# First four groups of a windowed-attention and MLP kernel in another order of work

## The chip, the cores and the metric

The kernel runs on one core of a Trainium2 chip: TensorE (PE in the profile, its weight loads PEld), VectorE (DVE), ScalarE (ACT), GpSimd (POOL), SyncE (SP, here only a DMA queue) and 16 DMA engines. The metric is device time of one execution in microseconds; the median of the runs is compared.

## The reference

Four sequences of 768 tokens, 8 heads of 64, attend causally to a window of 128 tokens and to the first 4 tokens of the sequence (the sinks). The result, 3072 tokens by 512, goes through two matrix products with a quick GELU between them. Input and output are float32.

```python
scores = scale * np.matmul(q, k.transpose(0, 1, 3, 2))
keep = is_sink | ((rel >= 0) & (rel < window))
scores = np.where(keep, scores, -1000000000.0)
a = np.exp(scores - np.max(scores, axis=-1, keepdims=True))
a = a / (np.sum(a, axis=-1, keepdims=True) + 1e-09)
x = np.matmul(a, v)              # then (tokens, heads * head_dim)
h = x @ w_in
return (h * (1.0 / (1.0 + np.exp(-1.702 * h)))) @ w_out
```

## The kernel before

The 3072 tokens are cut into 12 groups of 256 (three to a sequence, `NT`), a group into two blocks of 128 tokens, and the 8 heads into four pairs, `hp`. Everything is written for fp16 operands; loads on POOL's queue convert. The schedule is manual: each engine executes its instructions in the order in which the program text issues them, and waits by semaphores for tiles of other engines. So the order of the calls is the order of work, and a waiting instruction holds up all that follow on its engine or its queue.

For a group, the steps are functions of the same names as in the diff. `load_part` issues one of six loads on POOL (two each of q, k and v). `transposed_qk` brings q and k to the layout with features on partitions: groups 0 to 2 (`EARLY` is 3) by transposes on TensorE with copies by DVE and ACT, the others by one DMA transpose on SP's queue. `sinks` and `scores` are the first matmuls on it, `maxima` (DVE) merges the window's two blocks by a mask and takes row maxima, `weights` (ACT) are four exponentials, `weights_transposed` turns them (TensorE and a copy for groups 0 and 1, a DMA transpose on SP after that), `lower` (DVE) and `upper` (POOL) mask the two halves, `values` multiplies by v, and `normal` (DVE) divides. `sink_terms`, `sink_weights`, `sink_transposed` do the same for the sinks. `x_transposed` turns the result for the products: on TensorE for groups 0 and 1, by DMA for the others. `ahead(n, hp)` is `sinks` (for pair 0), `scores` and `maxima` of a pair.

The products are `hidden(g, F2)`, eight blocks of 8 matmuls, each followed by a GELU on ACT, and `o(g, i, parts)`, four quarters of four matmuls for each of two token blocks, ended by `out_store`. Exponentials and GELU need different tables on ACT, which loads one at each change.

PSUM has eight banks: tag `nat` holds two score tiles of two banks, `mm` two banks (products, some transposes), `av` two banks (values, sink scores, other transposes). A tile waits until the previous holder of its buffer has been read.

Before the main loop stand the attention of group 0 and, between its steps, most of that of group 1. The main loop then runs stage n: exponentials of group n and the output products of group n-2 with its last two pairs of scores, then the hidden products of group n-1 with, between them, the values of group n and the first scores of group n+1. The DMA transpose of q and k of group n+2 is issued in stage n; for n = 1, which has a form of its own (`first`), `transposed_qk(3)` closes the stage. The start of stage n in its common form:

```python
            if att:
                for hp in (0, 1):
                    weights(n, hp)
                    weights_transposed(n, hp)
            o(g2, 0, 0, 1, 2, 3)
...
                weights(n, 3)
                weights_transposed(n, 3)
                sink_weights(n)
                lower(n, 0)
                if n + 2 < NG:
                    transposed_qk(n + 2)
```

## Time and profile before

| what | us |
|---|---|
| median of 3 runs | 249.29 (248.48 to 249.64) |
| the profiled execution, its own time | 249.51 |
| span of its trace | 247.8 |
| TensorE busy in the span | 222.1 (90%) |
| DVE, ACT, POOL busy | 148.0, 154.3, 99.9 |

In the profile a row of the timeline gives the start, the duration, the engine, the line, the operation with its result and operands, and in square brackets the idle time before it and what ended it. Rows with the letter q behind an engine's name are its sequencer's, among them the issues of DMAs. A window's row gives, for a stretch of time, the length, the busy time of the chosen engine, the granted clock of TensorE (1.00 is full), how busy the DMA engines were and the GB/s that they moved.

### The profile page before, as it was taken

Reading aid. Unit: us, or ns where it says so; the run is one execution under the profiler, and the core shown is the slowest. Engines: PE = TensorE matmul, PEld = TensorE weight load, DVE = VectorE, ACT = ScalarE, POOL = GpSimd, SP = SyncE. Lnnn points to the kernel's source line nnn. Section 1 sums busy time; section 2 is a strip of 40 time slices with the busy share of each in tenths; the row PEclk is TensorE's granted clock in tenths of the full one; section 3 lists DMA queues with packets and bytes.
Section 4 is the critical chain, followed back from the end, with each engine's and each line's share of the span. In section 5 each row is a group of like instructions: output and inputs, shape, how many; then the busy total and the mean of one; then the engine's idle time right before and its main releaser. Section 6 shows DMA issues by size and latency. Waiting matters only on the chain.

```text
span 247.8 us, 5720 instructions
## 1 busy us (share of the span) xinstructions
PE 222.1 (90%) x2172; PEld 151.8 (61%) x2172; DVE 148.0 (60%) x390; ACT 154.3 (62%) x350; POOL 99.9 (40%) x152
## 2 busy tenths in 40 slices
PE   0654779699999999999999999999999999799993
PEld 0542559548748649558478477487485694594851
DVE  7679725847757478379577467586682783730101
ACT  2286476277667775875775776677668757751430
POOL 8988594407622616637235276156110210310000
PEclk9996559999999999999999999999999999999999
DMA  9999999999999999999989989999992513503102
GB/s 81 152 197 198 163 207 182 154 127 174 178 146 131 158 169 142 130 202 160 129 165 122 163 150 159 160 144 143 157 157 43 139 33 68 147 3 85 42 3 86
DMA packets 134668, 33.13 MB, mean 134 GB/s; under 512 B 127344, under 2 KB 131568, under 8 KB 134640
## 3 DMA queue, kind: packets, MB, share of 16 engines
q0 software_dynamic: 79104, 13.64, 72.6%
q1 hardware_dynamic: 55104, 18.99, 43.8%
q8 instruction: 17, 0.28, 0.5%
q10 hardware_dynamic: 432, 0.13, 0.2%
q14 instruction: 11, 0.09, 0.1%
HBM read 27.50 MB, written 6.29 MB: 136 GB/s over the span
## 4 chain that ended last, share of the span: by engine, by line
PE 63%; DMA 13%; DVE 10%; ACT 8%; issue 3%; SPq 2%; ACTq 0%; DVEq 0%
PE hT L387 30%; PE o L402 20%; DMA xT<-xn 9%; ACT A L251 4%; DVE m L236 3%; DVE nat L232 3%; PE nat L220 2%; DMA AT<-A 2%; PE av L339 2%; ACT L390 2%; PE av L327 2%; PE av L335 2%; PE tA L264 2%; DMA vsr<-in_v_dram 2%; SPq L424 1%
## 5 line engine op out<-in xcount | busy, mean ns | idle before, releaser
L387 PE MATMUL hT<-xT,w_in 128*128 128x256 f16 x768 | 95.5, 275 | 3.2 <-ACT gT L390 1.7
L402 PE MATMUL o<-w_out,gT 128*128 128x512 f16 x384 | 88.3, 380 | 0.0
L387 PEld LDWEIGHTS <-w_in 128*128 128x128 f16 x768 | 72.9, 99 | 16.4 <-DMA xT<-xn 2.6
L390 ACT ACTIVATE gT<-hT 128x512 f16<-128x512 f32 x96 | 56.2, 597 | 42.3 <-PE hT L387 42.2
L251 ACT ACTIVATE A<-nat,bias 128x128 f16<-128x128 f32 x192 | 53.8, 376 | 26.2 <-DVE bias L240 23.0
L313 POOL TENSOR_SCALAR_AFFINE_SELECT up<-AT 128x512 f16<-128x512 f16 (+1 forms) x48 | 28.0, 594 | 92.0 <-DMA AT<-A 86.8
L402 PEld LDWEIGHTS <-gT 128*128 128x128 f16 x384 | 35.2, 98 | 39.9
L232 DVE COPY_PREDICATED nat<-prev,nat 128x512 f32<-128x512 uint16 x48 | 33.2, 692 | 30.0 <-ACT A L251 13.1
L236 DVE TENSOR_REDUCE m<-nat 128x4 f32<-128x512 f32 x48 | 33.2, 691 | 1.6
L123 POOL DMA_DIRECT2D qkn<-in_q_dram x24 | 21.6, 910 | 5.0 <-DMA w_out<-in_moe_w_out_dram 3.3
L410 DVE COPY osb<-o 128x512 f32<-128x512 f32 x12 | 8.3, 690 | 23.7 <-PE o L402 23.7
L123 POOL DMA_DIRECT2D qkn<-in_k_dram x24 | 21.3, 895 | 1.9 <-DMA w_in<-in_moe_w_in_dram 1.6
L123 POOL DMA_DIRECT2D vn<-in_v_dram x24 | 21.3, 895 | 1.6 <-issue 1.1
L357 DVE TENSOR_TENSOR xn<-av,rcp 128x256 f16<-128x256 f32 x48 | 20.4, 424 | 1.7
L300 DVE TENSOR_TENSOR lo<-AT,own 128x512 f16<-128x512 f16 (+1 forms) x48 | 18.9, 413 | 2.1 <-DMA AT<-A 2.1
L335 PE MATMUL av<-vn,up 128*128 128x65 f16 x160 | 18.3, 195 | 0.0
L339 PE MATMUL av<-vn,lo 128*128 128x65 f16 x160 | 18.3, 196 | 0.0
L356 DVE RECIPROCAL rcp<-av 128x4 f32<-128x4 f32 x48 | 8.6, 179 | 14.6 <-PE av L339 14.4
L220 PEld LDWEIGHTS <-qkT 64*128 64x128 f16 x352 | 11.5, 99 | 8.5 <-issue 8.1
L327 PE MATMUL av<-vs,AsT 128*128 128x130 f16 x80 | 16.5, 224 | 0.0
L220 PE MATMUL nat<-qkT 64*128 64x128 f16 x288 | 16.0, 228 | 0.0
L335 PEld LDWEIGHTS <-up 128*128 128x128 f16 x160 | 14.8, 100 | 0.6 <-issue 0.2
(51 smaller groups left out, 168.2 us busy)
## 6 DMA issues: line engine op xcount, KB each, us to landing
out_dram<-osb SPq DMA_DIRECT2D x24, 256.0 KB
qkn<-in_q_dram POOLq DMA_DIRECT2D x24, 128.0 KB, 5.3
qkn<-in_k_dram POOLq DMA_DIRECT2D x24, 128.0 KB, 5.0
vn<-in_v_dram POOLq DMA_DIRECT2D x24, 128.0 KB, 5.5
w_in<-in_moe_w_in_dram POOLq DMA_DIRECT2D x4, 512.0 KB, 9.1
w_out<-in_moe_w_out_dram POOLq DMA_DIRECT2D x4, 512.0 KB, 10.6
AT<-A SPq DMA_TRANSPOSE x40
xT<-xn SPq DMA_TRANSPOSE x10
```

What stands on the lines that cost most here:

```text
L123: nc.gpsimd.dma_start(dst, (q, k, v)[e][b, :, rows].rearrange("h s d -> s h d"))
L220: nc.tensor.matmul(o, qkT[r, 0, i, hp], keys[r], start=True, stop=True)
L232: nc.vector.copy_predicated(out=nat[:, :, :, P:], mask=kinds(take_prev, g % NT), data=nat[:, :, :, 0:P])
L236: nc.vector.tensor_reduce(out=m1.rearrange("p h i -> p (h i)"), in_=nat.rearrange("p h i c -> p (h i) c")[:, :, P:], axis=AX.X, op=ALU.max,)
L251: nc.scalar.activation(out=A[:, 2 * h + i], in_=nat[:, h, i, P:], func=AF.Exp, bias=bias[:, i, hp, h : h + 1], scale=scale,)
L313: nc.gpsimd.affine_select(out=out, in_=in_, pattern=[[0, rows], [-1, P]], compare_op=ALU.is_gt, fill=zero_reg, base=0, channel_multiplier=1,)
L327: nc.tensor.matmul(av[:, i].rearrange("p h d -> p (h d)"), AsT, vs[b][:, c : c + 2].rearrange("p h d -> p (h d)"), start=True, stop=False,)
L335: nc.tensor.matmul(av[:, i, h], up[:, h, i], vn[b][J // 2][:, J % 2, head], start=False, stop=False)
L339: nc.tensor.matmul(av[:, i, h], own_w[:, h, i], vn[b][t][:, i, head], start=(I == 0), stop=(I == 0 or h == 1))
L387: nc.tensor.matmul(hT[:, f], w_in16[:, c, bass.ts(F, P)], xT[:, :, c], start=(c == 0), stop=(c == 3))
L390: nc.scalar.activation(out=G[g]["gT"][:, 2 * F2 : 2 * F2 + 2].rearrange("p f s -> p (f s)"), in_=hT.rearrange("p f i s -> p (f i s)"), fun ...
L402: nc.tensor.matmul(o, gT[:, F, bass.ts(i, P)], w_out16[:, F], start=(F == 0), stop=(F == NF - 1))
```

## The change

The main loop begins at group 3 (`EARLY`) and loses the form for n = 1. Ahead of it groups 0 to 2 are written out. Group 0's attention runs by itself until its x is transposed; the hidden products of group 0 carry the second half of group 1's q and k transposes and three pairs of its scores, those of group 1 the same for group 2. The third pair has its two halves in the two `av` banks, so that three pairs of scores wait for their exponentials at once. The output products of a group are cut into quarters with the next group's weights, values and normalisation between them. The exponentials and the scores of group 3 stand beside the output products of group 1, with group 2's values.

Group 1's weights are transposed on TensorE into score buffers, two pairs at a time. x of group 2 is transposed on TensorE. `lower` of the first two pairs of group 0 moves to POOL (`selected`). The `vs` and `vn` constants are set later, but for those of the first sequence and group. The first chunk of w_in is loaded ahead of group 1's q and k, the output weights after group 0's masks; the loads of groups 2 to 5 move as the diff shows. On SP's queue, q and k of group 3 are transposed behind `out_store` of group 0, those of groups 4 and 5 both behind the weights of group 3.

```diff
@@ -154,14 +154,14 @@
         else:
             for part in parts:
                 for a in (2 * part, 2 * part + 1):
-                    bank = mm_bank if g < 2 else av_bank
-                    tp = bank(f"tqk{g}_{a}", (P, HP, P), FP16)
+                    first = g == 0 or (g == 1 and part == 0)
+                    tp = (mm_bank if first else av_bank)(f"tqk{g}_{a}", (P, HP, P), FP16)
                     for c in range(HP):
                         nc.tensor.transpose(tp[:, c], n[:, a, bass.ts(c, P)], ident)
-                    if a % 2 == 0:
+                    if (g == 1 and part == 0) or (g != 1 and a % 2 == 1):
+                        nc.scalar.copy(T[:, bass.ts(a, HP)], tp)
+                    else:
                         nc.vector.tensor_copy(out=T[:, bass.ts(a, HP)], in_=tp)
-                    else:
-                        nc.scalar.copy(T[:, bass.ts(a, HP)], tp)
...
-        nat = psp.tile([P, 2, 2, 2 * P], FP32, tag="nat", bufs=2, name=f"nat{g}_{hp}")
+        if (g, hp) in ((1, 2), (2, 2)):
+            nat = [av_bank(f"nat{g}_{hp}_{h}", (P, 2, 2 * P)) for h in range(2)]
+        else:
+            whole = psp.tile([P, 2, 2, 2 * P], FP32, tag="nat", bufs=2, name=f"nat{g}_{hp}")
+            G[g]["whole", hp] = whole
+            nat = [whole[:, h] for h in range(2)]
...
-                    o = nat[:, h, i, bass.ts(part, P)]
+                    o = nat[h][:, i, bass.ts(part, P)]
...
     def maxima(g: int, hp: int):
         m1 = work.tile([P, 2, 2], FP32, tag="m1", name=f"m1{g}_{hp}")
+        if ("whole", hp) in G[g]:
+            nat = G[g]["whole", hp]
+        else:
+            for h, nat in enumerate(G[g]["nat", hp]):
+                nc.vector.copy_predicated(
+                    out=nat[:, :, P:], mask=kinds(take_prev, g % NT)[:, h], data=nat[:, :, 0:P]
+                )
+                nc.vector.tensor_reduce(out=m1[:, h], in_=nat[:, :, P:], axis=AX.X, op=ALU.max)
...
-    def weights_transposed(g: int, hp: int):
-        A = G[g]["A", hp]
+    def flat_weights(g: int, hp: int):
         AT = work.tile([P, 2, 2, P], FP16, tag="AT", bufs=6, name=f"AT{g}_{hp}")
-        flat = AT.rearrange("p h i s -> p (h i) s")
-        if g < 2:
+        G[g]["AT", hp] = AT
+        return AT.rearrange("p h i s -> p (h i) s"), G[g]["A", hp]
+
+    def weights_transposed(g: int, hp: int, copy=None):
+
+        flat, A = flat_weights(g, hp)
+        if copy is not None:
             tp = mm_bank(f"tA{g}_{hp}", (P, 4, P), FP16)
             for a in range(4):
                 nc.tensor.transpose(tp[:, a], A[:, a], ident)
-            if g == 0 or hp < 3:
-                nc.scalar.copy(flat, tp)
-            else:
-                nc.vector.tensor_copy(out=flat, in_=tp)
+            copy(flat, tp)
         else:
             nc.sync.dma_start_transpose(flat, A.rearrange("p a c -> p (a c)"))
-        G[g]["AT", hp] = AT
+
+    def two_weights_transposed(g: int, pairs, copy):
+
+        tp = psp.tile([P, 2, 8, P], FP16, tag="nat", bufs=2, name=f"tA{g}_{pairs[0]}")
+        for e, hp in enumerate(pairs):
+            flat, A = flat_weights(g, hp)
+            for a in range(4):
+                nc.tensor.transpose(tp[:, e, a], A[:, a], ident)
+            copy(flat, tp[:, e, 0:4])
+
+    def by_dve(out_, in_):
+        nc.vector.tensor_copy(out=out_, in_=in_)
+
+    def by_act(out_, in_):
+        nc.scalar.copy(out_, in_)
...
-    def lower(g: int, hp: int):
+    def lower(g: int, hp: int, pool=False):
 
         AT, i0 = G[g]["AT", hp], int(g % NT == 0)
         lo = work.tile([P, 2, 2, P], FP16, tag="lo", bufs=4, name=f"lo{g}_{hp}")
...
+        if pool:
+            selected(lo, AT, i0, 1)
+        else:
+            nc.vector.tensor_tensor(
+                out=lo[:, :, i0:], in0=AT[:, :, i0:], op=ALU.mult,
+                in1=own.unsqueeze(1).unsqueeze(1).broadcast_to((P, 2, 2 - i0, P)),
+            )
         G[g]["lo", hp] = lo
 
     def upper(g: int, hp: int):
         AT, i0 = G[g]["AT", hp], int(g % NT == 0)
         up = work.tile([P, 2, 2, P], FP16, tag="up", bufs=4, name=f"up{g}_{hp}")
+        selected(up, AT, i0, -1)
+        G[g]["up", hp] = up
+
+    def selected(to, AT, i0: int, sign: int):
...
+            out=out, in_=in_, pattern=[[0, rows], [sign, P]], compare_op=ALU.is_gt if sign < 0 else ALU.is_ge,
+            fill=zero_reg, base=0, channel_multiplier=-sign,
         )
...
-        if g < 2:
+        if g < EARLY:
...
-                if g == 0 or i == 0:
+                if i == 0:
                     nc.scalar.copy(xT[:, bass.ts(i, HP)], tp)
                 else:
                     nc.vector.tensor_copy(out=xT[:, bass.ts(i, HP)], in_=tp)
...
-    def out_store(g: int, i: int):
+    def out_store(g: int, i: int, act=False):
         b, t = divmod(g, NT)
         osb = work.tile([P, DM], FP32, tag="osb", bufs=3, name=f"osb{g}_{i}")
-        if i == 0:
+        if i == 0 or act:
             nc.scalar.copy(osb, G[g]["o", i])
         else:
             nc.vector.tensor_copy(out=osb, in_=G[g]["o", i])
...
-    for i in range(2):
-        for b in range(B):
+    for b in range(B):
+        for i in range(2):
             nc.sync.dma_start(vsr[bass.ts(i, 32), b], v[b, :, 0:n_sink])
     masked_l = const.tile([P, P], FP16, name="maskedl")
     masked_r = const.tile([P, P], FP16, name="maskedr")
+    sinkA = [const.tile([P, P], FP16, name=f"sinkA{i}") for i in range(2)]
+    nc.vector.memset(vs[0], 0.0)
+    nc.vector.tensor_copy(out=vs[0][:, :, D : D + 1], in_=sink_rows.unsqueeze(2))
     nc.vector.memset(masked_l, -1000.0)
-    for row in vn:
-        for t_ in row:
-            nc.vector.memset(t_[:, :, :, D : D + 1], 1.0)
-    sinkA = [const.tile([P, P], FP16, name=f"sinkA{i}") for i in range(2)]
-    for t_ in (*kd, *sinkA, *vs):
+    for t_ in (*kd, *sinkA):
         nc.vector.memset(t_, 0.0)
-    for t_ in vs:
-        nc.vector.tensor_copy(out=t_[:, :, D : D + 1], in_=sink_rows.unsqueeze(2))
+    nc.vector.memset(vn[0][0][:, :, :, D : D + 1], 1.0)
     zero_reg = nc.gpsimd.to_reg(0.0)
+    load_w_in(0)
     load_qk(1)
     load_v(0)
-    load_w_in(0)
-    load_w_in(1)
-    transposed_qk(0)
-    sink_keys(0, nc.vector.tensor_copy)
-    load_v(1)
-    load_w_in(2)
-    load_w_in(3)
-    load_qk(2)
+    for i in (1, 2, 3):
+        load_w_in(i)
+
+    def sink_columns(b: int):
+        nc.vector.memset(vs[b], 0.0)
+        nc.vector.tensor_copy(out=vs[b][:, :, D : D + 1], in_=sink_rows.unsqueeze(2))
...
+    transposed_qk(0, (0,))
+    sink_values(0)
+    transposed_qk(0, (1,))
+    sink_keys(0, nc.vector.tensor_copy)
     ahead(0, 0)
     ahead(0, 1)
     weights(0, 0)
-    transposed_qk(1, (0,))
     weights(0, 1)
-    transposed_qk(1, (1,))
     scores(0, 2)
+    weights_transposed(0, 0, by_act)
     maxima(0, 2)
-    weights_transposed(0, 0)
+    upper(0, 0)
+    lower(0, 0, pool=True)
+    weights(0, 2)
     scores(0, 3)
     maxima(0, 3)
     sink_terms(0)
-    weights(0, 2)
-    weights_transposed(0, 1)
+    weights_transposed(0, 1, by_act)
+    upper(0, 1)
+    lower(0, 1, pool=True)
+    sink_weights(0)
     weights(0, 3)
-    ahead(1, 0)
-    weights_transposed(0, 2)
-    sink_weights(0)
-    sink_values(0)
-    lower(0, 0)
-    lower(0, 1)
-    ahead(1, 1)
-    weights_transposed(0, 3)
     sink_transposed(0)
-    upper(0, 0)
-    upper(0, 1)
-    load_v(2)
+    weights_transposed(0, 2, by_dve)
+    lower(0, 2)
     upper(0, 2)
+    weights_transposed(0, 3, by_act)
+    values(0, 0)
+    values(0, 1)
+    transposed_qk(1, (0,))
+    normal(0, 0)
+    lower(0, 3)
     upper(0, 3)
+    normal(0, 1)
+    for hp in (2, 3):
+        values(0, hp)
+        normal(0, hp)
+    x_transposed(0)
     load_w_out(0)
     load_w_out(1)
-    lower(0, 2)
-    lower(0, 3)
+    load_v(1)
+    load_w_out(2)
+    load_w_out(3)
+    load_qk(2)
+
+
+    for F2 in range(NF // 2):
+        hidden(0, F2)
+        if F2 == 0:
+            transposed_qk(1, (1,))
+            for row in vn:
+                for t_ in row[int(row is vn[0]) :]:
+                    nc.vector.memset(t_[:, :, :, D : D + 1], 1.0)
+        if F2 in (1, 2, 3):
+            ahead(1, F2 - 1)
+
+
     weights(1, 0)
-    weights_transposed(1, 0)
     weights(1, 1)
-    weights_transposed(1, 1)
-    for hp in range(HP):
-        values(0, hp)
-        if hp == 1:
-            scores(1, 2)
-        if hp == 3:
-            scores(1, 3)
-        normal(0, hp)
-        if hp == 1:
-            maxima(1, 2)
-            weights(1, 2)
-    weights_transposed(1, 2)
-    x_transposed(0)
+    sink_columns(1)
+    o(0, 0, 0)
+    o(0, 1, 0)
+    scores(1, 3)
     maxima(1, 3)
     sink_terms(1)
+    o(0, 0, 1)
+    weights(1, 2)
+    two_weights_transposed(1, (0, 1), by_dve)
+    sink_weights(1)
     weights(1, 3)
-    weights_transposed(1, 3)
-    load_w_out(2)
-    load_w_out(3)
+    upper(1, 0)
+    upper(1, 1)
+    o(0, 1, 1)
+    sink_transposed(1)
+    lower(1, 0)
+    lower(1, 1)
+    o(0, 0, 2)
+    two_weights_transposed(1, (2, 3), by_act)
+    upper(1, 2)
+    upper(1, 3)
+    values(1, 0)
+    normal(1, 0)
+    values(1, 1)
+    lower(1, 2)
+    normal(1, 1)
+    o(0, 1, 2)
+    lower(1, 3)
+    values(1, 2)
+    normal(1, 2)
+    o(0, 0, 3)
+    values(1, 3)
+    normal(1, 3)
+    out_store(0, 0)
+    o(0, 1, 3)
+    x_transposed(1)
+    out_store(0, 1, act=True)
+    load_v(2)
     load_qk(3)
-
-    for n in range(1, NG + LAG2):
-        att, first = n < NG, n == 1
+    load_v(3)
+
+
+    for F2 in range(NF // 2):
+        hidden(1, F2)
+        if F2 in (0, 1):
+            transposed_qk(2, (F2,))
+        if F2 in (2, 3, 4):
+            ahead(2, F2 - 2)
+    transposed_qk(3)
+    sink_keys(1, nc.gpsimd.tensor_copy)
+
+
+    for hp in (0, 1):
+        weights(2, hp)
+        weights_transposed(2, hp)
+    sink_values(1)
+    o(1, 0, 0, 1, 2)
+    scores(2, 3)
+    maxima(2, 3)
+    sink_terms(2)
+    weights(2, 2)
+    weights_transposed(2, 2)
+    o(1, 0, 3)
+    out_store(1, 0)
+    ahead(3, 0)
+    load_part(4, 0)
+    upper(2, 0)
+    load_part(4, 1)
+    upper(2, 1)
+    o(1, 1, 0)
+    sink_weights(2)
+    weights(2, 3)
+    weights_transposed(2, 3)
+    lower(2, 0)
+    lower(2, 1)
+    load_part(4, 2)
+    upper(2, 2)
+    load_part(4, 3)
+    upper(2, 3)
+    o(1, 1, 1)
+    sink_transposed(2)
+    weights(3, 0)
+    weights_transposed(3, 0)
+    scores(3, 1)
+    lower(2, 2)
+    maxima(3, 1)
+    o(1, 1, 2)
+    for hp in (0, 1):
+        values(2, hp)
+        normal(2, hp)
+    scores(3, 2)
+    weights(3, 1)
+    weights_transposed(3, 1)
+    lower(2, 3)
+    values(2, 2)
+    normal(2, 2)
+    o(1, 1, 3)
+    out_store(1, 1, act=True)
+    values(2, 3)
+    normal(2, 3)
+    maxima(3, 2)
+    x_transposed(2)
+    scores(3, 3)
+    maxima(3, 3)
+    sink_terms(3)
+    weights(3, 2)
+    weights_transposed(3, 2)
+    weights(3, 3)
+    weights_transposed(3, 3)
+    sink_weights(3)
+    load_qk(5)
+    lower(3, 0)
+    transposed_qk(4)
+    transposed_qk(5)
+    sink_columns(2)
+    sink_columns(3)
+
+    for n in range(EARLY, NG + LAG2):
+        att = n < NG
...
+        if n > EARLY:
+            if att and n + 1 < NG and (n + 1) % NT == 0:
+                sink_keys((n + 1) // NT, nc.gpsimd.tensor_copy)
+            if n in (4, 5):
+                load_v(n)
             if att:
                 for hp in (0, 1):
...
-            if first:
-                upper(n, 2)
-                upper(n, 3)
-                load_v(3)
-                load_qk(4)
-                load_v(4)
-            else:
-                for part in range(4):
-                    if n + 3 < NG:
-                        load_part(n + 3, part)
-                    if part < 2:
-                        upper(n, 2 + part)
+            for part in range(4):
+                if n + 3 < NG:
+                    load_part(n + 3, part)
+                if part < 2:
+                    upper(n, 2 + part)
...
-                if first:
-                    lower(n, 0)
-            if first and F2 in (2, 3):
-                transposed_qk(2, (F2 - 2,))
-            if F2 == (6 if first else 1):
                 ahead(n + 1, 0)
-            if F2 == 1:
                 lower(n, 1)
-            if F2 == (7 if first else 1):
...
-            for hp, at in enumerate((4, 5, 6, 7) if first else (3, 4, 6, 7)):
+            for hp, at in enumerate((3, 4, 6, 7)):
                 if F2 == at:
...
-                    if not first and hp in (1, 2):
+                    if hp in (1, 2):
                         paced_load(n + 3, 3 + hp, n, hp)
         if att:
             x_transposed(n)
             if n + 1 < NG and (n + 1) % NT == 0:
                 sink_values((n + 1) // NT)
-            if first:
-                transposed_qk(3)
-
```

## Prediction

> **What bounds the kernel now.** I read the page first, then the chain of waits, then the timeline engine by engine for the first 95 us, and last the half-microsecond windows of DMA traffic.
>
> ```profile
> PE 222.1 (90%) x2172; PEld 151.8 (61%) x2172; DVE 148.0 (60%) x390; ACT 154.3 (62%) x350; POOL 99.9 (40%) x152
> PEclk9996559999999999999999999999999999999999
> PE hT L387 30%; PE o L402 20%; DMA xT<-xn 9%; ACT A L251 4%; DVE m L236 3%; DVE nat L232 3%; PE nat L220 2%; DMA AT<-A 2%; PE av L339 2%; ACT L390 2%; PE av L327 2%; PE av L335 2%; PE tA L264 2%; DMA vsr<-in_v_dram 2%; SPq L424 1%
> ```
>
> TensorE is the bound, and it is nearly full from the first product on; the only weak stretch is the head, at half clock from 20.8 to 37.6 us. So whatever time the change gains or loses lies ahead of a state that both kernels share. I take as that state the third pair of product blocks of group 2 (hidden(2, 2)). There both have finished the products of groups 0 and 1 and the weights of group 3, and both run the same loop afterwards. These rows of TensorE place the first product and that state:
>
> ```profile
> 34.27 3.54 PE L387 MATMUL hT<-xT,w_in 128*128 128x256 f16 x16
> ...
> 74.05 1.98 PE L387 MATMUL hT<-xT,w_in 128*128 128x256 f16 x16
> 75.92 0.34 PE L191 MATMUL sk<-kd,qkT 128*128 128x8 f16 x8
> 76.94 1.91 PE L387 MATMUL hT<-xT,w_in 128*128 128x256 f16 x16
> ```
>
> The reader is to see that hidden(0) starts at 34.27, hidden(2) at 74.05, the sink scores of group 4 at 75.92 without a wait, and the shared state at 76.94. The third is possible because the DMA transpose of group 4's q and k was issued a whole stage earlier, as SP's queue shows:
>
> ```profile
> 45.54 5.25 SPq L153 DMA_TRANSPOSE qkT<-qkn  x1
> 59.95 3.27 SPq L153 DMA_TRANSPOSE qkT<-qkn  x1
> 75.41 1.26 SPq L270 DMA_TRANSPOSE AT<-A  x1
> 76.89 3.48 SPq L153 DMA_TRANSPOSE qkT<-qkn  x1
> 181.51 3.02 SPq L153 DMA_TRANSPOSE qkT<-qkn  x1
> ```
>
> The rows are groups 3, 4, (the weights of a pair), 5 and 11. How long such a transpose takes to land is seen once, where POOL stood waiting for group 3's, and in the traffic of group 11's, when nothing else moved:
>
> ```profile
> 57.00 0.44 POOL L170 COPY kd<-qkT 64x16 f16<-64x16 f16 x2 [10.46 <-DMA qkT<-qkn]
> ...
> 54.50:55.00 0.50, 1.00 3.29 56
> 55.00:55.50 0.50, 1.00 0.04 3
> ...
> 185.00:185.50 0.50, 1.00 0.71 153
> 185.50:186.00 0.50, 1.00 0.00 0
> ```
>
> Last column GB/s: group 3's data stopped at 55.0 and POOL went on at 57.0, so 2.0 us pass from the last byte to the waiter; issue to waiter was 11.5 us under full loads. Group 11's ran from 181.5 to 185.4, 3.9 us to the last byte.
>
> **The change part by part.** I lay the new order out with the rows' durations: a pair's maxima 1.54 us on DVE; four exponentials 1.02 us, 1.14 to their end; a table load 1.28; eight product matmuls 0.87 at full clock and 1.66 at half; a quarter of an output product 0.86; a pair's scores 0.33; a pair's values 0.4; a normalisation 0.55; a copy out of PSUM 0.59 on ACT, 0.42 on DVE.
>
> Group 0 alone (to the first product). Gone from between its steps are group 1's q/k transposes and copies, two pairs of group 1's maxima on DVE and all of its weights. Scores (0,2) wait for the exponentials that end at 13.36 and start at 13.4 instead of 14.84; the last maxima end at 17.1, the last exponentials at 18.85, their transpose's copy at 19.8; values from 19.15, the four normalisations until 23.1, x transposed and copied until 24.3. The first product starts at 24.3 instead of 34.3, a lead of 10.0 us. The new prologue costs nothing: one vs memset of 0.93 us where four stood, ending before the first copy that waits for TensorE at 6.0; sink_values(0), 1.22 us, lies between two copies that start at 6.1 and 8.55. The two selections moved from DVE to POOL (0.4 us each) fit between POOL's issues. On the load queue the traffic rows give about 2.55 us per weight chunk and 0.85 us per q, k or v part, so w_in lands by 24.5, one chunk being needed at once, and w_out by 36.5, each quarter ahead of its use; q and k of group 2 by 40.
>
> Hidden(0) beside group 1's scores: 8 matmuls at half clock 1.66, eight transposes 1.04, 8 more 1.66, then 48 at full clock 5.2 and scores 1.2: until 35.1. The scores that wait in two half banks cost DVE four operations of an estimated 0.42 us (half the slope of the 0.69 us rows) for two of 0.69, 0.3 us behind the products. The eleven vn memsets (0.8 us) lie there too.
>
> Output(0) beside group 1's attention: two quarters to 36.9. Now scores (1,3) need the buffer that the first exponentials free: last gelu 35.8, table 37.1, exponentials 38.2. TensorE waits 1.4 us. From 38.3 its own work is 8.5 us (six quarters, 16 weight transposes, values, x), with 0.9 us of waits for exponentials, normalisations and xT's copy: hidden(1) starts at 47.7. Hidden(1) with group 2's transposes and scores: 9.6 us, 0.5 of it a wait for an ACT copy queued behind the table load: 57.35.
>
> Output(1) beside group 2's attention and group 3's scores. Here 6.9 us of products have two groups' maxima and exponentials to cover. Scores (2,3) wait for exponentials that end at 60.45 (0.5 us), scores (3,1) for 64.45 (0.5). DVE's work from 60.9 on adds to 12.7 us: five maxima 7.7, four masks 1.5, four normalisations 2.2, the rest 1.3. One of these masks (lo of pair 2) waits until 65.7 for its weights' transpose, issued at 62.6, by the 3.1 us of such a row (69.23 to 72.31), and three operations queue behind it. So TensorE waits 1.9 us at values (2,2) for a normalised bank, 0.8 for the last normalisation, 1.0 for xT's DVE copy, which stands behind the maxima (3,2). Hidden(2) starts at 73.15. Of the lead of 10.0 us 0.9 is left. A second count agrees: 7.3 us of waits against 2.4 before (46.3 to 48.75), 2.8 us of group 1's TensorE work that used to lie ahead of hidden(0), 0.45 for x of group 2 on TensorE, 1.0 more at half clock: 9.1.
>
> The transpose of group 4's q and k. It moves on SP's queue from behind group 2's last weights to behind group 3's. Maxima (3,3) end at 74.6, exponentials at 75.8, their DMA transpose issues 75.85 to 77.1, so this one issues at 77.25. It is needed at once: in the built order TensorE has only hidden(2, 0), hidden(2, 1) (until 74.9) and the sink transpose (76.0) ahead of the group 4 sink scores, whose weight load waits for it. Everything of TensorE is queued behind that wait, and DVE and ACT wait for TensorE. Its landing: at least 3.9 us (group 11's last byte), at most 11.5 (group 3, loads all along). Other groups' last bytes come 3.6 to 5.9 us after issue; few loads run here, so I take 4.9 plus the 2.0 us seen above, 6.9. Sink scores at 84.15, two pairs' scores to 84.9, the shared state at 84.9 against 76.94: +7.95 us.
>
> By the Trainium skill, "DMA: Bandwidth & Descriptors", Anatomy of one DMA, a transfer takes 2.0 us plus its bytes at 436 GB/s (measured there on GpSimd's path): for these 512 KB an estimate of 3.2 us, and the result would be about 255. The rows' 3.9 us to the last byte alone are longer, so the rows decide.
>
> The clock. TensorE would stand idle about 8 us.
>
> ```profile
> 20.00:21.00 1.00, 0.86 (x13) 0.76 1.35 224
> 36.00:37.00 1.00, 1.00 (x6) 0.50 1.23 211
> 38.00:39.00 1.00, 1.00 (x15) 1.00 1.24 207
> 47.00:48.00 1.00, 0.01 (x1) 1.00 2.43 154
> ```
>
> The fourth column is the granted clock. It fell at 20.8 after 3.6 us of little work, stayed at 1.00 through a hole of 2.4 us, and came back after about 4 us of full work, in which 16 matmuls took 3.33 us instead of 1.75: between 0 and 1.6 us lost. The hole is longer than either row's, so I take 1.6. "TensorE: Matmul & The Clock Gate", Part 1, speaks against the change too: cold after an idle window of about 3.4 us, warm after as much work, an estimate of 1.7 us lost; no row shows a full idle window of that length.
>
> After the state the loop is the same but for four v loads moved into it, on a queue with gaps, and sink columns (2.6 us of DVE) that lie in the hole; without the hole they would delay DVE by about 1 us and TensorE by little.
>
> Sum: 7.95 + 1.6 = +9.5 us. The profiled execution took 249.51 us (span 247.8), 0.2 above the median of 249.29; on the median the forecast is 258.8 us.
>
> **The rivals.** *A slow landing*: the transpose meets loads for groups 5 and 6 and takes group 3's 11.5 us: +12.5 + 1.6, 263.4. For it: POOL issues such loads between its selections here. Against: group 3's met eight parts, this meets two or three. *A quick landing*: 3.9 us in all and no lost clock: +5.0, 254.3. For it: group 11's row. Against: the 2.0 us to the waiter. *The lead survives*, faster: the place is DVE's chain beside output(1). If it is shorter than I lay it out, the exponentials (3,3) end earlier and everything after moves with them; with the landing as taken it decides when they end 8 us earlier, by 67.8 (9.5 with the clock). At 12 us earlier the result is 246.8. For it: hidden(0) does start 10 us sooner. Against: DVE alone has 12.7 us of rows between 60.9 and 74.6, and TensorE without any wait would reach the pair hidden(2, 1) at 66.5. That the order isn't what the text says is excluded by the built order of the engines.
>
> **How the numbers follow.** Forecast 0.66 (256 to 262, by landings of 5 to 8 us and a chain 1 us off), slow landing 0.12, quick landing 0.12, lead survives 0.07, about no change 0.03. The range 253.5 to 263.6 takes the first three and leaves out 0.1 and some tails. Faster by over 0.5% 0.07, within it 0.03, slower 0.90; 0.5% (1.2 us) is about what a measurement of this kernel can tell.
>
> **What would show it.** Right: the first product near 24; waits of TensorE at scores (1,3), values (2,2); hidden(2) near 73; then a hole of some 8 us before the group 4 sink scores, ended by the DMA qkT<-qkn, with SP issuing that transpose after the last weights of group 3; the clock at 0.5 for about 4 us afterwards. Wrong: hidden(2) before 66, or the sink scores without a wait.

## The result and the profile after

The changed kernel takes 267.96 us (median of 4 runs, 266.0 to 269.21); the kernel before took 249.46 us on the same chip. The ratio is 1.072, with a 95% interval of 1.062 to 1.083. So it is slower, as forecast, but by 18 us where 9.5 were worked out. 267.96 lies above the whole range of 253.5 to 263.6. Here and below a ratio leaves out executions more than 1.5% above the fastest of the same kernel, while medians and ranges are of all.

The profiled execution after the change, the longest of the four, has a span of 267.5 us. First the lines of its page for the engines, the clock by 40 slices, and the chain by lines:

```profile
PE 228.4 (85%) x2180; PEld 155.7 (58%) x2180; DVE 150.5 (56%) x394; ACT 154.4 (58%) x350; POOL 100.5 (38%) x152
PEclk9999979999965659999999999999999999999999
PE hT L421 26%; PE o L436 14%; ACT A L263 5%; DVE nat L239 5%; DVE m L242 5%; DMA AT<-A 4%; DMA vn<-in_v_dram 3%; DMA xT<-xn 3%; DMA qkT<-qkn 3%; ACT L424 2%; ACT L263 2%; PE nat L225 2%; PE av L373 2%; DMA qkn<-in_q_dram 2%; PE av L361 2%
```

The weak stretch is no longer at the head but in two places up to 100 us, where the clock is down. Two new links of the chain matter here: group 4's `qkT<-qkn`, which was forecast, and `vn<-in_v_dram`, which was not. (`hT` has moved from L387 to L421, `o` from L402 to L436, the scores from L220 to L225.)

The timeline of TensorE, with what ended each wait in brackets:

```profile
24.85 1.86 PE L421 MATMUL hT<-xT,w_in 128*128 128x256 f16 x8 [0.61 <-DVE xT L407]
...
33.68 0.21 PE L225 MATMUL nat<-qkT,qkT 64*128 64x128 f16 x1 [1.96 <-DVE sn L200]
33.99 5.33 PE L421 MATMUL hT<-xT,w_in 128*128 128x256 f16 x32
39.16 1.89 PE L436 MATMUL o<-w_out,gT 128*128 128x512 f16 x8
42.46 0.23 PE L225 MATMUL nat<-qkT,qkT 64*128 64x128 f16 x2 [1.41 <-ACT A L263]
...
45.23 0.38 PE L291 MATMUL tA<-ident,A 128*128 128x128 f16 x4 [1.18 <-DVE AT L295]
...
48.35 0.38 PE L291 MATMUL tA<-ident,A 128*128 128x128 f16 x4 [0.73 <-ACT AT L298]
...
54.00 1.05 PE L421 MATMUL hT<-xT,w_in 128*128 128x256 f16 x8 [0.52 <-DVE xT L407]
...
64.05 2.75 PE L436 MATMUL o<-w_out,gT 128*128 128x512 f16 x12
...
82.90 3.47 PE L421 MATMUL hT<-xT,w_in 128*128 128x256 f16 x16 [0.60 <-DVE xT L407]
93.93 0.38 PE L191 MATMUL sk<-kd,qkT 128*128 128x8 f16 x8 [7.51 <-DMA qkT<-qkn]
95.21 3.59 PE L421 MATMUL hT<-xT,w_in 128*128 128x256 f16 x16
```

The reader is to set the starts beside the forecast: hidden(0) 24.85 (24.3), output(0) 39.16 (35.1), hidden(1) 54.00 (47.7), output(1) 64.05 (57.35), hidden(2) 82.90 (73.15), shared state 95.21 (84.9). In the kernel before, the state was at 76.94. So 18.27 us were lost ahead of it, and 1.4 after it: 267.5 − 95.21 = 172.3 us against 247.8 − 76.94 = 170.9.

The first excess comes before output(0). DVE's row there, and SP's queue at the end of the region:

```profile
32.68 0.68 DVE L546 MEMSET vn<- 128x16 f16 x8 [4.65 <-DMA vn<-in_v_dram]
33.33 0.30 DVE L200 TENSOR_SCALAR sn<-sk 128x64 f32<-128x64 f32 x1
```

```profile
83.81 3.14 SPq L283 DMA_TRANSPOSE AT<-A  x2
87.17 7.33 SPq L153 DMA_TRANSPOSE qkT<-qkn  x2
```

DVE stood for 4.65 us at the memset of a `vn` tile, until a load of v had landed. Everything that group 1 needs of DVE was queued behind it: first the sink scores' scaling (L200), which TensorE then waited for. The second fence shows the forecast part: the transpose of group 4's q and k was issued at 87.17 behind group 3's last weights, and TensorE's sink scores started at 93.93, 6.76 us later.

### The profile page after: what moved, and what is told of

It is laid out like the page before. It is cut to its first block, busy times and chain, and to the rows that moved or that the text cites. A ratio compares the mean times of both kernels' runs of the same rounds, so it can differ in the third digit from the quotient of the medians.

```text
span 267.5 us, 5739 instructions
## 1 busy us (share of the span) xinstructions
PE 228.4 (85%) x2180; PEld 155.7 (58%) x2180; DVE 150.5 (56%) x394; ACT 154.4 (58%) x350; POOL 100.5 (38%) x152
## 4 chain that ended last, share of the span: by engine, by line
PE 50%; DVE 15%; DMA 15%; ACT 13%; issue 4%; POOL 1%; SPq 1%; ACTq 0%; DVEq 0%; POOLq 0%
PE hT L421 26%; PE o L436 14%; ACT A L263 5%; DVE nat L239 5%; DVE m L242 5%; DMA AT<-A 4%; DMA vn<-in_v_dram 3%; DMA xT<-xn 3%; DMA qkT<-qkn 3%; ACT L424 2%; ACT L263 2%; PE nat L225 2%; PE av L373 2%; DMA qkn<-in_q_dram 2%; PE av L361 2%
## 5 line engine op out<-in xcount | busy, mean ns | idle before, releaser
L421 PE MATMUL hT<-xT,w_in 128*128 128x256 f16 x768 | 100.2, 284 | 4.0 <-DVE xT L407 1.7
L436 PE MATMUL o<-w_out,gT 128*128 128x512 f16 x384 | 90.0, 382 | 0.0
L421 PEld LDWEIGHTS <-w_in 128*128 128x128 f16 x768 | 75.1, 102 | 19.7 <-issue 2.5
L436 PEld LDWEIGHTS <-gT 128*128 128x128 f16 x384 | 35.1, 98 | 39.0 <-issue 0.6
L239 DVE COPY_PREDICATED nat<-prev,nat 128x512 f32<-128x512 uint16 x46 | 31.8, 692 | 29.8 <-PE nat L225 20.0
L242 DVE TENSOR_REDUCE m<-nat 128x4 f32<-128x512 f32 x46 | 31.8, 691 | 1.6
L444 DVE COPY osb<-o 128x512 f32<-128x512 f32 x10 | 6.9, 692 | 22.7 <-PE o L436 22.5
L369 PE MATMUL av<-vn,up 128*128 128x65 f16 x160 | 19.0, 199 | 0.0
L225 PEld LDWEIGHTS <-qkT 64*128 64x128 f16 x352 | 11.8, 100 | 11.0 <-issue 10.8
L225 PE MATMUL nat<-qkT 64*128 64x128 f16 x288 | 16.4, 230 | 0.0
```

Source lines behind the costliest of these rows:

```text
L225: nc.tensor.matmul(o, qkT[r, 0, i, hp], keys[r], start=True, stop=True)
L239: nc.vector.copy_predicated(out=nat[:, :, :, P:], mask=kinds(take_prev, g % NT), data=nat[:, :, :, 0:P])
L242: nc.vector.tensor_reduce(out=m1.rearrange("p h i -> p (h i)"), in_=nat.rearrange("p h i c -> p (h i) c")[:, :, P:], axis=AX.X, op=ALU.max,)
L369: nc.tensor.matmul(av[:, i, h], up[:, h, i], vn[b][J // 2][:, J % 2, head], start=False, stop=False)
L421: nc.tensor.matmul(hT[:, f], w_in16[:, c, bass.ts(F, P)], xT[:, :, c], start=(c == 0), stop=(c == 3))
L436: nc.tensor.matmul(o, gT[:, F, bass.ts(i, P)], w_out16[:, F], start=(F == 0), stop=(F == NF - 1))
```

## The experiments

Each ratio is to the kernel before on the same chip: 249.84 us in the first four runs, 250.45 in the next four (two transposes, mask, quarter, one call of before), 249.9 in the last three. Line numbers of `hT` and what follows shift by one where an edit adds a line.

### The memsets of vn in the prologue

Theory: the memset that writes the ones column of group 1's v tile comes, in program order, after the load into that tile, so it must wait for it. The load stands behind w_out's parts 0 and 1 on POOL's queue. Rival: TensorE's wait of 1.96 us is one of DVE's maxima, and would stand without the memsets.

```diff
-    nc.vector.memset(vn[0][0][:, :, :, D : D + 1], 1.0)
+    for row in vn:
+        for t_ in row:
+            nc.vector.memset(t_[:, :, :, D : D + 1], 1.0)
...
         if F2 == 0:
             transposed_qk(1, (1,))
-            for row in vn:
-                for t_ in row[int(row is vn[0]) :]:
-                    nc.vector.memset(t_[:, :, :, D : D + 1], 1.0)
```

> The changed kernel, with the twelve constants of the v tiles set ahead of all loads, as before, instead of beside the first hidden products. In its trace DVE stands 4.65 us at the second of them, until group 1's v has landed at 32.6 us; TensorE has a hole of 1.96 us there and runs 32 product matmuls at half clock from 34.9 to 38.6 us. Theory: all of this goes, about 2.0 us of hole and 1.7 us of half clock, and the time falls from 268.0 to about 264.2 us, with the clock at 1.00 from 29 to 70 us. Rival, the output stage behind it takes the gain back because it waits for exponentials anyway: 266.5 to 268.

Measured: 261.97 us (258.98 to 263.32), ratio to before 1.041 (1.029 to 1.052). On the ratios it gains 3.15% of 249.5, 7.9 us, but this ratio rests on two of the four executions; on the medians it gains 6.0. The timeline of TensorE, from an execution of 263.11 us:

```profile
31.79 3.67 PE L421 MATMUL hT<-xT,w_in 128*128 128x256 f16 x32
35.30 1.89 PE L436 MATMUL o<-w_out,gT 128*128 128x512 f16 x8
...
78.32 1.92 PE L421 MATMUL hT<-xT,w_in 128*128 128x256 f16 x16 [1.08 <-DVE xT L407]
...
86.87 0.38 PE L191 MATMUL sk<-kd,qkT 128*128 128x8 f16 x8 [5.33 <-DMA qkT<-qkn]
```

The hole is gone, the 32 product matmuls take 3.67 us instead of 5.33, and output(0) starts at 35.30, 0.2 from the forecast of 35.1. The rival falls. The sink scores of group 4 come 7.1 us sooner than in the changed kernel: 3.9 from the hole and its clock, 0.7 in output(1), and 2.5 because the transpose, issued here at 82.59, took 4.3 us instead of 6.76 to its waiter. Only the 3.9 us are traced to the memsets, as the theory had them (3.8). The other 3.2 us are not: nothing had changed in the transpose's place in the order, and yet it landed sooner.

### Group 4's q and k early, alone and with the memsets

Theory: the wait for group 4's transpose costs about 8 us, and goes if that transpose is issued behind group 3's first weights, with the loads moved ahead of it.

```diff
     load_v(3)
+    load_qk(4)
...
     weights_transposed(3, 0)
+    transposed_qk(4)
     scores(3, 1)
...
-    transposed_qk(4)
     transposed_qk(5)
```

(The four `load_part(4, ...)` further down are left out accordingly.)

> The changed kernel, with group 4's q and k loaded directly behind group 3's v and transposed on SP's queue behind the first weights of group 3 instead of behind the last. Theory: the wait of 7.5 us ahead of group 4's sink scores goes, the first GELU of group 2 (87.7 us) is the next bound, so the third block pair starts 7.4 us earlier, and with TensorE not idle the clock is back sooner, 1.7 us: 268.0 falls to about 259. Rival, the hole only hid other work (2.6 us of sink columns on DVE, the table load, the weights' transposes that are now later on SP): 262 to 264.

> The changed kernel with both edits: constants of the v tiles ahead of all loads, and group 4's q and k loaded and transposed earlier. Theory: the two places are independent and the gains add, 3.8 + 9.1 us: about 255 us, still slower than before by 5 to 6 us, because output(1) has two groups' attention to cover. Rival, one of the two hides behind the other: 258 to 260.

Measured: alone 259.49 us (257.79 to 260.93), ratio 1.039 (1.030 to 1.048); with both edits 255.16 us (252.99 to 256.61), ratio 1.021 (1.012 to 1.030). In the ratios the steps are 3.3% alone and 2.0% on top of the memsets, where the landing was quicker. With this edit alone the shared state is reached at 86.99, 8.2 us sooner than in the changed kernel, and the clock has only its first dip. The memset's row shows that it is the landing of the load that counts. In this execution hidden(0) ran at full pace from 23.94 on, so DVE and TensorE came sooner to the same stop, and stood longer (first DVE's row, then TensorE's):

```profile
33.58 0.68 DVE L546 MEMSET vn<- 128x16 f16 x8 [7.59 <-DMA vn<-in_v_dram]
34.58 0.26 PE L225 MATMUL nat<-qkT,qkT 64*128 64x128 f16 x1 [5.32 <-DVE sn L200]
```

### The reverse: the kernel before with that transpose late

This takes the transpose of group 4's q and k out of its early place in the kernel before and leaves everything else.

```diff
-                if n + 2 < NG:
+                if n == 3:
+                    transposed_qk(4)
+                if n > 2 and n + 2 < NG:
                     transposed_qk(n + 2)
```

> The kernel before, with one thing alone: the DMA transpose of group 4's q and k is issued behind the last weights of group 3 (where the changed kernel has it) instead of one stage earlier. Theory: it is issued at 76.8 us instead of 59.95, lands 6.8 us later, so the sink scores move from 75.9 to about 83.6 and the third block pair of group 2 from 76.9 to 84.4; with 1.7 us of half clock behind the hole the time goes from 249.5 to about 258.5 us. Rival, quick landing (3.9 us in all, no lost clock): 254.

Measured: 259.3 us (258.55 to 260.4), ratio 1.039 (1.032 to 1.046), 9.7 us. Its TensorE rows, and SP's:

```profile
75.09 1.98 PE L387 MATMUL hT<-xT,w_in 128*128 128x256 f16 x16
76.90 0.22 PE L290 MATMUL tAs<-ident,sinkA 128*128 128x128 f16 x1
84.61 0.38 PE L191 MATMUL sk<-kd,qkT 128*128 128x8 f16 x8 [7.49 <-DMA qkT<-qkn]
...
85.89 3.59 PE L387 MATMUL hT<-xT,w_in 128*128 128x256 f16 x16
```

```profile
77.91 7.39 SPq L153 DMA_TRANSPOSE qkT<-qkn  x2
```

Issue to waiter 6.70 us, the hole 7.49 against 7.51 in the changed kernel, the products behind it at half clock (3.59 us for 16). The state is 8.95 us later than in the kernel before; 0.9 of that is there at hidden(0) already (35.16 against 34.27), ahead of the edit, and behind the state 1.0 us more is lost. So the trace puts the step at some 9.1 us and the ratio at 7.9 to 11.5. This is the sum of the prediction, 9.5 us, met alone in a kernel that has no other part of the change. The rest of the changed kernel's loss, about as much, must then come from elsewhere.

### The transposes of two pairs into one tile

In output(0), the changed kernel turns the weights of two pairs into the halves of one PSUM tile, each pair's four transposes followed by its copy. TensorE's rows at 45.23 and 48.35 wait for the copy of the first half before the second half is written.

```diff
-        for e, hp in enumerate(pairs):
-            flat, A = flat_weights(g, hp)
+        both = [flat_weights(g, hp) for hp in pairs]
+        for e, (flat, A) in enumerate(both):
             for a in range(4):
                 nc.tensor.transpose(tp[:, e, a], A[:, a], ident)
+        for e, (flat, A) in enumerate(both):
             copy(flat, tp[:, e, 0:4])
```

> This is the changed order with the twelve vn memsets in the prologue and group 4's q and k loaded and transposed early (255.16 us), and in addition the eight transposes of group 1's pairs 0 and 1 are all issued on TensorE ahead of the two copies out of their common PSUM tile. Theory (the two stops of TensorE in output(0), 1.18 us behind the first DVE copy and 0.73 us behind the first ACT copy, come from writing a tile that a copy is still reading): both stops go, 1.9 us earlier at hidden(1) and at the shared state, about 253.3 us. Rival (output(0) is paced by ACT's exponentials, and TensorE only waits somewhere else in it): the stops reappear at the values of group 1, 255.2 us, no change.

Measured: 253.28 us, ratio 1.0135 (1.0085 to 1.0186); run a second time, 251.65 us, ratio 1.009 (1.006 to 1.013). Without this edit it was 1.021 (1.012 to 1.030), so the intervals overlap, and the trace has to decide. Both stops are gone:

```profile
38.93 1.04 PE L437 MATMUL o<-w_out,gT 128*128 128x512 f16 x4
39.81 0.61 PE L291 MATMUL tA<-ident,A 128*128 128x128 f16 x8
40.25 1.03 PE L437 MATMUL o<-w_out,gT 128*128 128x512 f16 x4
...
42.26 0.61 PE L291 MATMUL tA<-ident,A 128*128 128x128 f16 x8
```

From output(0) to hidden(1) it is 12.83 us (35.30 to 48.13) where the changed kernel takes 14.84, and so does the kernel with both edits (33.69 to 48.53). So 2.0 us of output(0) were these copies, and the rival is out.

### A mask behind the maxima; the mask again; a quarter earlier

Theory: DVE's queue stands at the mask of group 2's pair 2 for its DMA transpose, and the normalisations behind it are late for TensorE's values (2,2).

```diff
     scores(3, 1)
-    lower(2, 2)
     maxima(3, 1)
...
     weights_transposed(3, 1)
+    lower(2, 2)
     lower(2, 3)
```

> As the run before it, and the mask of group 2's pair 2 (DVE) stands behind the maxima of group 3's pair 1 and the weights of that pair instead of ahead of them, so that the DVE queue doesn't stand at that mask for its DMA transpose. Theory (the head of DVE's queue waits for the landing, and the maxima and normalisations behind it are late for that): the wait of 2.4 us that TensorE has at values (2,2) goes for the most part, 1.7 to 2.4 us, about 251.3 us. Rival (DVE's rows beside output(1) add up to the time there, whatever their order): the idle time moves to another place in output(1), about 253.3 us.

Measured: 251.8 us (249.87 to 253.68), ratio 1.0055 (1.002 to 1.009), which agrees with the theory's number. The trace does not agree: from output(1) to hidden(2) it is 17.10 us here and 17.08 without the edit, and the 1.7 us between the two profiles arise before output(0), where this execution has its first products at full pace. So the pair was run again on one chip, with a third kernel, in which the next edit below is kept and the mask put back.

> The kernel of e4 once more, next to the two below, because the profile of e6 shows output(1) as long as that of e4 (17.10 against 17.08 us) although the medians differ by 1.5 us, and the head of the two profiles differs by 1.7 us of clock. If the mask's place is worth time: e6 below this by 1 us or more. If the difference came from the clock of the head in the executions drawn: within 0.6 us of e6, both near 252.4 us.

> The kernel of e6 once more. If the mask's place is worth time, 1 us or more below e4_again; if not, within 0.6 us of it.

> The kernel of e7 with the mask of pair 2 back ahead of the maxima of pair 1 of group 3. If the mask's place is worth time, 1.0 to 1.5 us above e7's 251.7, some 253 us; if not, the values (2,2) wait about 1.8 us in one piece where e7 has 0.71 and 0.98, and the time is that of e7 within 0.6 us.

Measured: 251.65 and 251.69 us, ratios 1.009 (1.006 to 1.013) and 1.0035 (0.999 to 1.008); the third 252.52 us, ratio 1.007 (1.003 to 1.012). By the ratios of the pair the mask's place is worth 0.6%, 1.5 us, with intervals that overlap; by the medians nothing. The waits of TensorE did change; here they are without the edit and with it, from the second runs:

```profile
69.42 0.23 PE L362 MATMUL av<-vs,AsT 128*128 128x130 f16 x1 [2.41 <-DVE xn L392]
...
73.77 3.08 PE L422 MATMUL hT<-xT,w_in 128*128 128x256 f16 x16 [1.07 <-DVE xT L408]
78.66 1.91 PE L422 MATMUL hT<-xT,w_in 128*128 128x256 f16 x16 [0.61 <-ACT gT L425]
```

```profile
67.17 0.23 PE L362 MATMUL av<-vs,AsT 128*128 128x130 f16 x1 [0.76 <-DVE xn L392]
68.05 0.20 PE L374 MATMUL av<-vn,lo 128*128 128x65 f16 x1 [0.62 <-DVE lo L331]
...
72.31 1.92 PE L422 MATMUL hT<-xT,w_in 128*128 128x256 f16 x16 [1.07 <-DVE xT L408]
...
77.20 3.08 PE L422 MATMUL hT<-xT,w_in 128*128 128x256 f16 x16 [0.94 <-ACT gT L425]
```

A wait of 2.41 us becomes two of 1.38 in all: about 1 us in the second pair of profiles, nothing in the first. What the edit is worth stays open between 0 and 1.5 us. The third kernel has 2.45 us in one piece there. Its ratio, 1.007, is that of its counterpart with the mask moved (1.007, below; 252.52 against 251.74 us, on another chip), which speaks for nothing gained but doesn't settle it.

The last edit of this group fills TensorE's wait at scores (1,3) with a quarter that is ready, and gives the second copy of group 2's transposed x to ACT.

```diff
     o(0, 1, 0)
+    o(0, 0, 1)
     scores(1, 3)
...
-    o(0, 0, 1)
...
-                if i == 0:
+                if i == 0 or g == 2:
                     nc.scalar.copy(xT[:, bass.ts(i, HP)], tp)
```

> As the run before it, and the quarter o(0,0,1) stands ahead of scores (1,3), and the second copy of group 2's transposed x is made by ACT instead of DVE. Theory (TensorE stands 1.4 us at scores (1,3) with a ready quarter of 0.9 us behind it, and 0.8 us at hidden(2) for a copy queued behind maxima on DVE): 0.9 and 0.4 us less, about 250 us, level with the kernel before (249.8). Rival (the exponentials of pair 3 and the copies on ACT come later by the same amount and end the region): 251 to 252 us.

Measured: 251.74 us (251.01 to 253.38), ratio 1.007 (1.003 to 1.010): no gain over the kernel without the edit, as the rival had it. The timeline says why:

```profile
38.45 0.23 PE L225 MATMUL nat<-qkT,qkT 64*128 64x128 f16 x2 [0.55 <-ACT A L263]
...
39.48 0.61 PE L291 MATMUL tA<-ident,A 128*128 128x128 f16 x8 [0.63 <-ACT A L263]
...
41.17 0.23 PE L318 MATMUL tAs<-ident,sinkA 128*128 128x128 f16 x1 [0.23 <-DVE AT L296]
...
74.45 1.91 PE L422 MATMUL hT<-xT,w_in 128*128 128x256 f16 x16 [0.61 <-ACT xT L406]
...
79.48 3.39 PE L422 MATMUL hT<-xT,w_in 128*128 128x256 f16 x16 [0.94 <-ACT gT L425]
```

One wait of 1.41 us has become three of 0.55, 0.63 and 0.23, the same 1.41, and from output(0) to hidden(1) it is 12.84 us (35.14 to 47.98) against 12.83. Two of the three waits end with ACT's exponentials, so these seem to set the end, not TensorE's order. And hidden(2) waits 0.46 us less for x, but the state comes 5.03 us after it instead of 4.88: TensorE then waits 1.21 us for the sink weights and 0.94 for the first GELU. On ACT both stand behind the exponentials of pair 3, which waited 0.48 us for DVE's maxima.

### One call of the kernel before

The hole of the kernel before, from 46.3 to 48.75 us, ends with a wait of 1.74 us for a normalisation behind the maxima of group 2's pair 1. The edit lets those follow the last normalisations.

```diff
-            if F2 == (7 if first else 1):
+            if F2 == 1 and not first:
                 ahead(n + 1, 1)
...
+            if first and F2 == 7:
+                ahead(n + 1, 1)
```

> The kernel before, with one call moved: in stage 1 the scores and maxima of group 2's pair 1 stand behind the values and normalisations of the last two pairs of group 1 instead of ahead of them. Theory (the hole of TensorE from 46.3 to 48.75 us waits for normalisations that stand behind those maxima, 1.54 us, on DVE): the hole shrinks by about 1.5 us, about 248.3 us. Rival (the exponentials of that pair come later by as much and hold up the output products of stage 2): 249.8 us, no change.

Measured: 248.55 us (247.04 to 250.38) against 250.45, ratio 0.994 (0.991 to 0.998). It is the only kernel of this study that is faster than the one before, by 0.2 to 0.95%. The wait is down from 1.74 to 0.21 us, and the shared state comes at 76.28 instead of 76.94, although hidden(0) starts 0.67 us later in this execution (34.94; its first 16 products then make up 0.35 of that):

```profile
46.99 0.34 PE L369 MATMUL tx<-ident,xn 128*128 128x128 f16 x3 [0.30 <-DVE xn L357]
47.53 0.45 PE L369 MATMUL tx<-ident,xn 128*128 128x128 f16 x5 [0.21 <-DVE xn L357]
47.82 3.62 PE L402 MATMUL o<-w_out,gT 128*128 128x512 f16 x16
```

## Why the prediction was half right

**What held.** The first product starts at 24.85 against a forecast of 24.3, the lead of 10 us exists, and it is given back before hidden(2). The wait at scores (1,3) is 1.41 us (1.4). The transpose of group 4 issues 4.3 us after hidden(2) starts (4.1) and takes 6.76 us to its waiter (6.9), and the hole is 7.51 us (some 8). Behind the state 1.4 us are lost (1.6 for the clock). Put into the kernel before by itself, this one step costs 9.7 us: the 9.5 of the sum. That the landing was met so closely is in part luck: with the memsets in the prologue the same transpose, behind the same weights, took 4.3 us. The estimate of 3.2 us by "DMA: Bandwidth & Descriptors" of the Trainium skill, Anatomy of one DMA, is below every issue-to-waiter time of such a transpose looked at in these kernels: 4.3 us is the shortest, and 6.76 the one that counted.

**What failed.** The sum was the hole and its clock alone, on the ground that the lead is nearly used up by hidden(2): 73.15 against 74.05 in the kernel before. In fact hidden(2) starts at 82.90, 8.85 us behind. By the starts of TensorE's rows the layout missed 10.3 us ahead of the state, 0.55 of them before the first product:

| step, as the prediction put it | forecast | after | missed |
|---|---|---|---|
| end of hidden(0): "The eleven vn memsets (0.8 us) lie there too" | 35.1 | 39.16 | 4.1 |
| output(0): "0.9 us of waits for exponentials, normalisations and xT's copy" | 12.6 | 14.84 | 2.2 |
| hidden(1) | 9.65 | 10.05 | 0.4 |
| output(1): waits of 4.7 us in all | 15.8 | 18.85 | 3.0 |
| hidden(2) to the state | 11.75 | 12.31 | 0.6 |

The first is the step that failed most plainly. The memsets were costed by their duration, 0.8 us, and laid beside products. One of them writes into a tile that a load, issued before it, was still filling, though other columns of it; so it waited, 4.65 us, and it stood at the head of DVE's queue. The load's place could be estimated ahead of time from the prediction's own numbers: w_in by 24.5, two chunks of w_out at 2.55 us, two parts of v at 0.85 and 2.0 us to the waiter make 33.3; it landed at 32.6. The prediction never asked where group 1's v stood in that queue. The hole then took the clock down: 32 matmuls in 5.33 us instead of 3.67. Without it output(0) starts 0.2 us from the forecast, in an execution whose first products ran at the slow pace that was forecast; in executions at full pace it starts at 32.9 to 33.7.

The second is a term left out: the two stops of 1.18 and 0.73 us for copies out of a tile shared by two pairs. Taking them out gave 2.0 us in the trace.

The third, output(1), is a size, and not that of the waits. TensorE was idle there for 4.88 us, against 4.7 forecast, though the parts were others: 1.59 and 1.50 us at the values, not one wait of 1.9, and the mask that DVE stood at (1.79 us) was that of pair 1, not pair 2. Its work was mis-sized: it was busy for 13.97 us where the forecast leaves 11.1 (15.8 less 4.7). From 75.9 us on TensorE ran at half clock, which the prediction had only behind the state. In windows of 1 us (the fourth column of numbers is the granted clock):

```profile
75.00:76.00 1.00, 0.60 (x16) 0.93 1.00 219
76.00:77.00 1.00, 0.00 (x0) 0.50 1.20 132
77.00:78.00 1.00, 0.90 (x11) 0.50 2.14 134
```

The same stretch takes 16.86 us in the kernel with group 4's q and k early, where the clock stayed at 1.00: 12.00 busy and 4.86 idle. So 2 of the 3.0 us go with the clock, and most of the rest is work of TensorE that the forecast put too low (12.0 against 11.1). Why the clock fell there and not in that kernel, whose loads stand elsewhere, no run here told.

**The rivals.** Slow and quick landing did not happen. The lead did not survive. Repairing the two losses that were not foreseen and the one that was still leaves the changed order between 251.7 and 253.3 us, level with the kernel before at best (ratio 1.0035 with 0.999 to 1.008). The reason that was given for that, DVE's chain beside output(1) with too few products over it, is consistent with the waits for `xn` and `xT` left in those profiles. It was not tested by itself, and there is another wait in output(1) that nobody forecast: TensorE's sink scores of group 3 wait 0.5 to 1.4 us, in the kernels with a tile's transposes ahead of its copies, for POOL's copy of the sink keys (`kd`), which itself waits for the DMA transpose of group 3's q and k.

## What to carry to other kernels

An instruction that writes part of a tile has the cost of its wait, not of its duration: when a memset or a copy is moved, look for the loads and copies on that same tile, other columns of it included, that now come before it in program order, and read where they land. A lead at the head of a schedule is worth nothing by itself; follow it to the next state that both versions share, and check which transfers were issued early enough only because of the old order. To fill a wait with ready work helps only if that engine, and not the one it waits for, sets the end.

## What was not expected of the hardware

The clock fell behind shorter gaps than the rows of before suggested. In the changed kernel TensorE had done 0.72 us of work between 31 and 32, none in the next microsecond, 0.32 in the third:

```profile
31.00:32.00 1.00, 0.72 (x7) 1.00 1.43 201
32.00:33.00 1.00, 0.00 (x0) 1.00 1.24 208
33.00:34.00 1.00, 0.32 (x8) 1.00 1.24 205
34.00:35.00 1.00, 1.00 (x12) 0.95 1.25 208
35.00:36.00 1.00, 1.00 (x7) 0.50 1.25 203
```

The clock was granted at 0.50 from about 34.9 to 38.3, when TensorE was already busy again. In the kernel before it stayed at 1.00 through a hole of 2.4 us. (The fall that the prediction puts at 20.8 us was at 20.5.) "TensorE: Matmul & The Clock Gate" of the Trainium skill, Part 1, speaks of an idle window of about 3.4 us that runs freely. The gap ahead of this dip was 1.96 us, so by that rule there would have been none; the hole of 7.51 us, which is longer, did bring the clock from 1.00 to 0.50, at 89.5.

The granted clock does not tell the whole pace either. The first eight products of hidden(0) took 1.86 us in the changed kernel and 1.03 in the one with both edits (memsets, group 4 early), at the same place in the program and with 1.00 granted in both. Here are the windows from 24 to 26 us, first of the one, then of the other:

```profile
24.00:26.00 2.00, 1.39 (x9) 1.00 1.13 176
```

```profile
24.00:26.00 2.00, 1.39 (x18) 1.00 1.17 187
```

The kernel with group 1's transposes ahead of the copies, run twice, showed both paces (hidden(0) to output(0) in 10.48 and in 8.92 us), so 1.6 us of a single profile can come from this alone.
